# Memory attention, a mixing MLP and a gated MLP on one core: the first MLP's float64-formatted weights unpacked with one mask, the source order of the head rewritten, and the second batch's attention given later slots

## The chip, the cores and the metric

The kernel runs on one core of a Trainium2 chip. The metric is the device time of one execution in microseconds. Every time below is from the profile of one execution or from the runs of the kernel before.

## The reference, cut to what matters

Three stages follow each other, in float32, for 8 batches of 576 positions. The weights reach the chip as the 64-bit words of float64 arrays.

```python
# attention, 8 heads of 64, 32 memory slots
a = softmax(phi, axis=memory)
k_m, v_m = a.T @ k, a.T @ v                  # per head: 32 x 64
x = softmax(q @ k_m.T / 8) @ v_m             # back to 576 x 512
# first MLP
xk = mu_k * x + (1 - mu_k) * x_prev          # x_prev: the position before
xr = mu_r * x + (1 - mu_r) * x_prev
x2 = sigmoid(xr @ w_r) * (relu(xk @ w_k) ** 2 @ w_v)
# second MLP, gated over positions
h = relu(x2 @ w_in); u, v = halves(h)
out = (u * (w_spatial @ layer_norm(v) + b)) @ w_out
```

## The kernel before

**Units of work.** A batch is two attention steps (four heads each; `att_step(i)`, batch `i // 2`) and two blocks of the first MLP (288 positions each; the loop over `i` in `range(2 * B)`). A block has a K phase (8 output chunks `m`, with `w_k`), an R phase (4 chunks, with `w_r`) and a V phase (4 chunks, with `w_v`). Every product of the MLPs is made as three products of float32r halves (`three`, `gemm`, line 96), so each operand is split in a high and a low part: `split` (lines 103 and 104), a copy on ScalarE and a subtraction on VectorE. `prep_x` mixes a position with the one before it and splits the result (lines 374, 378, 103, 104).

**Weights.** `load_f64` loads 128 x 512 of the 64-bit words into a stage buffer and makes float32 of them; one such load is called a unit here. `w_k` is 8 units, `w_r` 4, `w_v` 8. There are four stage buffers in turn (`st0`, `st1`, and two halves of the tile `xT1`), and a load waits until the unit that used its buffer is done. A unit is: ScalarE scales the upper word in place (line 123); the last bits of the lower word go into place, on ScalarE in units 1 to 6 (line 127), by a shift on VectorE from unit 7 on (line 129); VectorE writes the sign into a byte (line 131) and joins both words (line 135); then a copy on ScalarE (line 141) and a subtraction on VectorE (line 142) make the two halves.

**Order.** The string `ORDER` writes the head of the kernel: `A I C K M B D L Q R q r` are loads of the first two attention steps, `w` is one unit of `w_k` (its load and its unpacking), and `a` and `b` are one stage each of attention steps 0 and 1. Behind it the four `prep_x` of block 0's K phase are made. `FIRST_BLOCK` does the same behind each chunk of block 0: `r` and `v` are units of `w_r` and `w_v`, `x` one `prep_x` of block 0's R phase. The source order is no fixed order of the engines: a planner of the framework lays out each engine's queue before the run, and takes the earliest in the source among the instructions that are ready by its own estimate. So the source order acts as a priority. Within an engine, and in SP's queue of DMA issues, the order laid out is then kept.

**Later attention.** Steps 2 to 15 are one generator, `att`; `pump`, called 20 times a block (a slot), takes pieces of it: none in slots 0 to 6, two a slot up to slot 31, then one. A step has 20 pieces. Steps 2 to 15 share one set of buffers (`space`), and step `i` issues the loads of step `i + 1` in its 12th piece. `prep_x` of a batch's first block runs in the R and V phases of the block before it.

Of the kernel before, what the change touches and what calls it, by code (L numbers as in the profile page):

```python
# [8 lines left out]
F32 = mybir.dt.float32  # L9
F32R = mybir.dt.float32r  # L10
U32 = mybir.dt.uint32
U8 = mybir.dt.uint8
ACTF = mybir.ActivationFunctionType
ALU = mybir.AluOpType
# [5 lines left out]
DM, DFF = 512, 1024  # L20
# [8 lines left out]
KC = DM // 128  # L29
# [1 line left out]

ORDER = "AICKMBDwLQRwwqwraaawaaabbbabaabbwbbwbw"


FIRST_BLOCK = ["arxxab", "b", "rxabr", "xab", "", "", "", "rv", "vvvv", "v", "", "vv"]
# [3 lines left out]
def kernel(  # L41
# [18 lines left out]
    nc = tc.nc  # L60
    scale = 1.0 / float(D) ** 0.5
# [5 lines left out]
    def tile_of(tag, shape, dtype=F32):  # L67
        return sb.tile(shape, dtype, tag=tag, name=tag)
# [16 lines left out]
    def pair(tag, shape):  # L85
        return tile_of(tag + "h", shape, F32R), tile_of(tag + "l", shape, F32R)

    def operand(n):

        return tile_of(f"xs{n}", [128, 2 * HB if n == 7 else 4 * HALF], F32R)  # L90
# [11 lines left out]
    def split(x, h, lo):  # L102
        nc.scalar.activation(out=h, in_=x, func=ACTF.Copy)  # L103
        nc.vector.tensor_tensor(out=lo, in0=x, in1=h.bitcast(F32), op=ALU.subtract)  # L104

    stages = []
    units = [0]

    def load_f64(src, wh=None, wl=None, raw=None):


        c, f = src.shape[1], src.shape[2] // 2
        buf = stages.pop(0)
        stages.append(buf)
        if isinstance(buf, str):
            buf = tile_of(buf, [128, 1024], U32)
        st = buf[:, 0:2 * c * f].rearrange("p (c f b) -> p c f b", c=c, b=2)
        nc.sync.dma_start(out=st.rearrange("p c f b -> p c (f b)"), in_=src)
        low, top = st[:, :, :, 0], st[:, :, :, 1]
        by = buf.bitcast(U8)[:, 0:8 * c * f].rearrange("p (c f b) -> p c f b", c=c, b=8)  # L120


        nc.scalar.activation(out=top.bitcast(F32), in_=top.bitcast(F32), func=ACTF.Copy, scale=2.0**-112)
        units[0] += 1
        if units[0] <= 6:

            nc.scalar.activation(out=low, in_=by[:, :, :, 3], func=ACTF.Copy, scale=2.0**-5, bias=-0.4999)
        else:
            nc.vector.tensor_scalar(out=low, in0=low, scalar1=29, scalar2=None, op0=ALU.logical_shift_right)

        nc.vector.tensor_scalar(  # L131
            out=by[:, :, :, 3], in0=by[:, :, :, 7], scalar1=128.0, scalar2=128.0, op0=ALU.is_ge, op1=ALU.mult
        )
        out = top if raw is None else raw.bitcast(U32)
        nc.vector.scalar_tensor_tensor(  # L135
            out=out, in0=top, scalar=3, in1=low, op0=ALU.logical_shift_left, op1=ALU.bitwise_or
        )
        v = out.bitcast(F32)
        if wh is None:
            return v  # L140
        nc.scalar.activation(out=wh, in_=v, func=ACTF.Copy)  # L141
        nc.vector.tensor_tensor(out=wl, in0=v, in1=wh.bitcast(F32), op=ALU.subtract)

    def weight(src, dst, n_c, width):

        chunks = src.bitcast(U32).rearrange("(c p) f -> p c f", p=128)
        for f0 in range(0, width, 128):
            for c in range(0, n_c, 4):
                load_f64(
                    chunks[:, c:c + 4, 2 * f0:2 * f0 + 256],  # L150
                    dst[0][:, c:c + 4, f0:f0 + 128], dst[1][:, c:c + 4, f0:f0 + 128],
                )
                yield
# [16 lines left out]
    def att_space(f, q, o, n, w, r):  # L170

        ns = SimpleNamespace(q=q)
        at = [0]

        def cut(t, n):
            at[0] += n
            return t[:, at[0] - n:at[0]]

        ns.kv = cut(f, NT * HG * KV).rearrange("p (t j c) -> p t j c", t=NT, j=HG)
        ns.ph = cut(f, NT * 128).rearrange("p (t m) -> p t m", t=NT)  # L180
        ns.pT = cut(f, S)
        ns.kmT = cut(f, 128)
        at[0] = 0
        ns.st = cut(o, S).rearrange("p (a m) -> p a m", m=32)
        ns.at = cut(o, S)
        at[0] = 0
        ns.vb = cut(w, 256).rearrange("p (j d) -> p j d", j=HG)
        at[0] = 0
        ns.km = cut(n, 128)
        ns.mx, ns.rs = cut(n, 1), cut(n, 1)  # L190
        ns.mx2, ns.sm = (cut(n, NBLK).rearrange("p (a m) -> p a m", m=1) for _ in range(2))
        at[0] = 0
        ns.vbh, ns.vbl = (cut(r, 256).rearrange("p (j d) -> p j d", j=2) for _ in range(2))
        ns.ats = cut(r, 2 * S).rearrange("p (j s) -> p j s", j=2)
        return ns
# [161 lines left out]
    def pump():  # L357
        n = slot[0]
        slot[0] += 1
        for _ in range(0 if n < 7 else 2 if n < 32 else 1):  # L360
            next(att, None)
        next(more[0], None)

# [5 lines left out]
    def prep_x(i, which, c):  # L369
        b, hf = divmod(i, 2)  # L370
        x32 = tile_of(next(x32_tags), [128, HB])
        n = which * KC + c

        nc.scalar.activation(
            out=x32, in_=xT[b][:, c, hf * HB:(hf + 1) * HB], func=ACTF.Copy,
            scale=mu_sb[:, 2 * KC + n:2 * KC + n + 1],
        )
        nc.vector.scalar_tensor_tensor(  # L378
            out=x32, in0=xT[b][:, c, 1 + hf * HB:1 + (hf + 1) * HB], scalar=mu_sb[:, n:n + 1], in1=x32,
            op0=ALU.mult, op1=ALU.add,  # L380
        )
        both = operand(n)[:, 0:2 * HB]
        h, lo = both[:, 0:HB], both[:, HB:]
        split(x32, h, lo)
        xs[i, which, c] = (h, lo)

    q_and_more = tile_of("ATl", [128, 4096])
    q0 = q_and_more[:, 0:HG * HB].rearrange("p (j s) -> p j s", j=HG)
    q1 = tile_of("kh", [128, HG, HB])
    n_r = 2 * HG * 64 + 2 * S  # L390
    rest = q_and_more[:, HG * HB:]
    spaces = [
        att_space(
            tile_of("ATh", [128, 4096]), q0, rest[:, 0:2 * S], rest[:, 2 * S:2 * S + 256],
# [8 lines left out]
    stages += ["st0", "st1"] + [spare[:, n, :] for n in range(2)]  # L403
    wk = pair("W1", [128, KC, DFF])
    wr = pair("W2", [128, KC, DM])
    w_k_steps = weight(w_k, wk, KC, DFF)
    w_r_steps = weight(w_r, wr, KC, DM)

    def load(n, i, late):
        dst, src = operands(i)[n + late]  # L410
        nc.sync.dma_start(out=dst, in_=src)
# [4 lines left out]
    def stage(steps):  # L416
        while not next(steps, True):
            pass

    for c in ORDER:  # L420
        if c == "w":
            next(w_k_steps)
        elif c in "ab":
            stage(first[c == "b"])
        elif c == "I":
            nc.sync.dma_start(out=ident_sb, in_=ident)
        elif c == "M":
            nc.sync.dma_start(out=mask_sb, in_=blockmask)
            nc.sync.dma_start(out=mu_sb[:, 0:2 * KC], in_=mu)
            nc.vector.tensor_scalar(  # L430
                out=mu_sb[:, 2 * KC:], in0=mu_sb[:, 0:2 * KC], scalar1=-1.0, scalar2=1.0,
                op0=ALU.mult, op1=ALU.add,
            )
        else:
            n, late = "ACKQBDLR".index(c.upper()), c.islower()
            load(n % 4, n // 4, late)
    for c in range(KC):
        prep_x(0, 0, c)

    wv = []  # L440

# [22 lines left out]
    def w_in_steps():  # L464
# [17 lines left out]
        for half in range(2):  # L482
            for j in range(2):
                load_f64(part(0, half, j), raw=quads[:, half, :, 128 * j:128 * j + 128])
                yield
                yield
# [4 lines left out]
        for j in range(2):  # L491
            at = []
            for half in range(2):
                at.append(load_f64(part(1, half, j)))
                yield
            (a11, a12), (a21, a22) = ((v[:, 0:2], v[:, 2:4]) for v in at)
            h, lo = (p[:, :, :, 128 * j:128 * j + 128] for p in wi_v)
            raw = room[:, 0:768].rearrange("p (q c f) -> p q c f", q=3, c=2)
            add(raw[:, 0], a21, a22, ALU.add)
            add(raw[:, 1], raw[:, 0], a11)  # L500
            add(raw[:, 2], a11, a21)
            for q, a in ((0, a11), (1, a12), (2, a22), (3, raw[:, 0]), (4, raw[:, 1]), (5, raw[:, 2])):
                split(a, h[:, q], lo[:, q])
                if q % 2:
                    yield
            add(raw[:, 0], a12, raw[:, 1])
            split(raw[:, 0], h[:, 6], lo[:, 6])
            yield
# [107 lines left out]
    for i in range(2 * B):  # L616
# [47 lines left out]
        for m in range(KC):  # L664
# [13 lines left out]
            n = HB if hf == 0 else 2 * HALF - HB  # L678
# [317 lines left out]
```

## Time and profile before

| | us |
|---|---|
| median of 3 runs (lowest, highest) | 1038.59 (1038.25, 1040.73) |
| profiled execution | 1039.12 |
| its span | 1037.3 |
| TensorE (PE) busy, share of the span | 989.4, 95% |
| VectorE (DVE) busy | 693.3, 67% |
| ScalarE (ACT) busy | 605.5, 58% |

The span runs from the first to the last instruction of the profile; the execution's own time is 1.82 us longer. PE's granted clock was at full speed in nearly the whole span. An engine's busy time counts overlapping instructions once.

### The profile page before, as it was taken

Reading aid. Unit: us, or ns where it says so; the run is one execution under the profiler, and the core shown is the slowest. Engines: PE = TensorE matmul, PEld = TensorE weight load, DVE = VectorE, ACT = ScalarE, POOL = GpSimd, SP = SyncE. Lnnn points to the kernel's source line nnn. Section 1 sums busy time; section 2 is a strip of 40 time slices with the busy share of each in tenths; the row PEclk is TensorE's granted clock in tenths of the full one; section 3 lists DMA queues with packets and bytes.
Section 4 is the critical chain, followed back from the end, with each engine's and each line's share of the span. In section 5 each row is a group of like instructions: output and inputs, shape, how many; then the busy total and the mean of one; then the engine's idle time right before and its main releaser. Section 6 shows DMA issues by size and latency. Waiting matters only on the chain.

```text
span 1037.3 us, 20311 instructions
## 1 busy us (share of the span) xinstructions
PE 989.4 (95%) x8080; PEld 957.8 (92%) x8080; DVE 693.3 (67%) x1558; ACT 605.5 (58%) x1287; POOL 117.3 (11%) x128
## 2 busy tenths in 40 slices
PE   3698999999999999999999999899999999999998
PEld 1387899999999999999999999899999999999998
DVE  3999956755674566567588557885665757575653
ACT  2797875675676568566766574655353534445342
POOL 0000000000000000000013022232232313132220
PEclk9999999999999999999999999899999999999999
DMA  9856622321332233223042212112110111111101
GB/s 258 260 155 205 203 80 64 113 88 55 108 111 88 58 110 105 75 66 105 7 145 64 74 44 84 39 55 65 36 61 30 59 35 53 40 59 46 54 24 46
DMA packets 67454, 88.94 MB, mean 86 GB/s; under 512 B 9504, under 2 KB 61088, under 8 KB 65312
## 3 DMA queue, kind: packets, MB, share of 16 engines
q1 hardware_dynamic: 67360, 87.65, 27.2%
q8 instruction: 63, 1.03, 0.4%
q14 instruction: 31, 0.25, 0.1%
HBM read 68.75 MB, written 18.87 MB: 84 GB/s over the span
## 4 chain that ended last, share of the span: by engine, by line
PE 81%; DVE 9%; DMA 4%; ACT 4%; issue 1%; SPq 1%; POOL 0%; ACTq 0%; POOLq 0%; DVEq 0%
PE bank L96 78%; PE bank L235 2%; DMA ATl<-in_qT 1%; DMA st<-in_w_in 1%; PE bank L285 1%; DVE xs L104 1%; DVE kl L104 1%; DMA ATh<-in_kv 1%; DVE st L131 1%; DVE xT L135 1%; DMA st<-in_w_v 0%; DVE xT L131 0%; ACT st L750 0%; ACT xs L103 0%; POOL st L558 0%
## 5 line engine op out<-in xcount | busy, mean ns | idle before, releaser
L96 PE MATMUL bank<-xs,W1h 128*128 128x288 f32 (+1 forms) x1496 | 251.9, 295 | 9.8 <-ACT xs L103 8.6
L96 PEld LDWEIGHTS bank<-xs,W1h 128*128 128x128 f32 x1496 | 214.4, 190 | 15.1 <-ACT xs L103 10.4
L96 PE MATMUL bank<-xs,W1l 128*128 128x288 f32 (+1 forms) x748 | 136.9, 292 | 0.0
L104 DVE TENSOR_TENSOR kl<-t,kh 128x576 fp32r<-128x576 f32 x64 | 49.1, 767 | 110.4 <-ACT kh L103 109.7
L96 PEld LDWEIGHTS bank<-xs,W1l 128*128 128x128 f32 x748 | 112.3, 190 | 0.0
L630 ACT ACTIVATE t<-bank 128x288 f32<-128x288 f32 x128 | 51.6, 403 | 78.3 <-PE bank L96 77.4
L767 DVE TENSOR_TENSOR st<-bank,st 128x256 f32<-128x256 f32 x90 | 37.5, 424 | 73.5 <-PE bank L96 64.9
L96 PE MATMUL bank<-kh,W3h 128*128 128x288 f32 x512 | 78.9, 295 | 6.2 <-ACT W3h L141 5.0
L96 PE MATMUL bank<-xs,W2h 128*128 128x288 f32 x512 | 84.2, 300 | 0.0
L96 PE MATMUL bank<-kh,W3l 128*128 128x288 f32 x512 | 81.3, 297 | 0.0
L96 PE MATMUL bank<-ATh,xs 128*128 128x256 f32 x472 | 75.1, 281 | 3.2 <-ACT st L770 3.1
L96 PEld LDWEIGHTS bank<-kh,W3h 128*128 128x128 f32 x512 | 71.1, 188 | 7.4 <-ACT W3h L141 5.9
L96 PE MATMUL bank<-kl,W3h 128*128 128x288 f32 x512 | 77.7, 294 | 0.0
L96 PEld LDWEIGHTS bank<-kh,W3l 128*128 128x128 f32 x512 | 71.3, 188 | 6.2 <-issue 6.0
L96 PEld LDWEIGHTS bank<-xs,W2h 128*128 128x128 f32 x512 | 72.6, 188 | 2.4 <-ACT t L630 2.2
L96 PEld LDWEIGHTS bank<-kl,W3h 128*128 128x128 f32 x512 | 71.0, 188 | 0.0
L96 PEld LDWEIGHTS bank<-ATh,xs 128*128 128x128 f32 x472 | 64.6, 191 | 3.7 <-ACT st L770 3.3
L104 DVE TENSOR_TENSOR xs<-st,xs 128x512 fp32r<-128x512 f32 x56 | 52.3, 935 | 16.1 <-ACT xs L103 16.1
L103 ACT ACTIVATE xs<-st 128x512 fp32r<-128x512 f32 x56 | 34.2, 630 | 46.0 <-POOL st L558 35.5
L103 ACT ACTIVATE kh<-bank 128x288 fp32r<-128x288 f32 x64 | 25.9, 406 | 50.9 <-DVE bank L887 50.9
L908 ACT ACTIVATE o<-bank 128x288 f32<-128x288 f32 x64 | 25.8, 404 | 45.2 <-PE bank L96 38.2
L331 POOL MEMSET xT<- 128x4 f32 x8 | 0.8, 105 | 445.0 <-DVE x32b L378 353.8
(242 smaller groups left out, 2217.4 us busy)
## 6 DMA issues: line engine op xcount, KB each, us to landing
ATh<-in_kv SPq DMA_DIRECT2D x15, 1300.0 KB, 6.1
out_T<-o SPq DMA_DIRECT2D x64, 144.0 KB, 1.7
ATl<-in_qT SPq DMA_DIRECT2D x30, 288.0 KB, 4.3
st<-x2d SPq DMA_DIRECT2D x32, 256.0 KB, 3.4
ATh<-in_phin SPq DMA_DIRECT2D x15, 320.0 KB, 3.0
x2d<-o SPq DMA_DIRECT2D x32, 144.0 KB, 2.0
ATh<-in_phiT SPq DMA_DIRECT2D x15, 288.0 KB, 2.8
st<-in_w_in SPq DMA_DIRECT2D x8, 512.0 KB, 4.0
```

Of the source, the lines that this page charges most:

```text
L96: nc.tensor.matmul(out=out, lhsT=pairs[i][0], rhs=pairs[i][1], start=i == 0, stop=i == n - 1)
L103: nc.scalar.activation(out=h, in_=x, func=ACTF.Copy)
L104: nc.vector.tensor_tensor(out=lo, in0=x, in1=h.bitcast(F32), op=ALU.subtract)
L131: nc.vector.tensor_scalar(out=by[:, :, :, 3], in0=by[:, :, :, 7], scalar1=128.0, scalar2=128.0, op0=ALU.is_ge, op1=ALU.mult)
L135: nc.vector.scalar_tensor_tensor(out=out, in0=top, scalar=3, in1=low, op0=ALU.logical_shift_left, op1=ALU.bitwise_or)
L235: nc.tensor.matmul(out=kvp[32 * j:32 * j + 32, :], lhsT=ph[:, t, 32 * j:32 * j + 32], rhs=kv[:, t, j, :], start=(t == 0), stop=(t == NT - 1),)
L285: nc.tensor.matmul(out=scs[hf][32 * j:32 * j + 32, :], lhsT=kmT[64 * hf:64 * hf + 64, 32 * j:32 * j + 32], rhs=q[64 * hf:64 * hf + 64, j, ...
L331: nc.gpsimd.memset(xT[b][:, :, 0:1], 0.0)
L630: nc.scalar.activation(out=ks[:, m % 2 * HB:(m % 2 + 1) * HB], in_=acc, func=ACTF.Relu)
L767: engine.tensor_tensor(out=dst, in0=x, in1=y, op=ALU.add)
L908: nc.scalar.activation(out=o, in_=acc, func=ACTF.Copy)
```

## The change

Three edits, with block 0's tables (`FIRST_BLOCK`) left as they are.

1. `load_f64` is cut in two: `fetch` issues the load, the rest unpacks. In units 1 to 20 (all of `w_k`, `w_r`, `w_v`) the scaled upper word now goes into one of two separate tiles (`moved`, in free room of `ATl`); ScalarE writes the last bits, as a byte, into the lowest byte of the upper word; and one VectorE mask keeps sign and last bits of that word at once. The join takes the scaled copy and the masked word. Later units (`w_in`, `w_out`) are made as before.
2. `ORDER` now issues four loads of `w_k` with the attention loads (`W`), then holds the stages of attention steps 0 and 1, then the four `prep_x` (`x`) between their last stages, and behind all of that the eight unpackings (`w`), each of which issues one more load.
3. `pump` takes no attention pieces in slots 0 to 16, and then three a slot up to slot 31.

```diff
-ORDER = "AICKMBDwLQRwwqwraaawaaabbbabaabbwbbwbw"
+ORDER = "AICKMBDWLQRWWWqraaabbbaabababaaxxbbbxxwwwwwwww"
...
+    def fetch(src):
...
+        return buf, st, c, f
+
+    def load_f64(src, wh=None, wl=None, raw=None):
+        buf, st, c, f = src if isinstance(src, tuple) else fetch(src)
         low, top = st[:, :, :, 0], st[:, :, :, 1]
...
-        nc.scalar.activation(out=top.bitcast(F32), in_=top.bitcast(F32), func=ACTF.Copy, scale=2.0**-112)
         units[0] += 1
-        if units[0] <= 6:
-            nc.scalar.activation(out=low, in_=by[:, :, :, 3], func=ACTF.Copy, scale=2.0**-5, bias=-0.4999)
+        if units[0] <= 20:
+            t = moved[units[0] % 2].rearrange("p (c f) -> p c f", c=c)
+            nc.scalar.activation(out=t, in_=top.bitcast(F32), func=ACTF.Copy, scale=2.0**-112)
+            nc.scalar.activation(out=by[:, :, :, 4], in_=by[:, :, :, 3], func=ACTF.Copy, scale=2.0**-5, bias=-0.4999)
+            nc.vector.tensor_scalar(
+                out=top, in0=top, scalar1=0x80000007 - 2**32, scalar2=None, op0=ALU.bitwise_and
+            )
+            t, low = t.bitcast(U32), top
         else:
+            t = top
+            nc.scalar.activation(out=top.bitcast(F32), in_=top.bitcast(F32), func=ACTF.Copy, scale=2.0**-112)
             nc.vector.tensor_scalar(out=low, in0=low, scalar1=29, scalar2=None, op0=ALU.logical_shift_right)
-        nc.vector.tensor_scalar(
-            out=by[:, :, :, 3], in0=by[:, :, :, 7], scalar1=128.0, scalar2=128.0, op0=ALU.is_ge, op1=ALU.mult
-        )
+            nc.vector.tensor_scalar(
+                out=by[:, :, :, 3], in0=by[:, :, :, 7], scalar1=128.0, scalar2=128.0, op0=ALU.is_ge, op1=ALU.mult
+            )
         out = top if raw is None else raw.bitcast(U32)
         nc.vector.scalar_tensor_tensor(
-            out=out, in0=top, scalar=3, in1=low, op0=ALU.logical_shift_left, op1=ALU.bitwise_or
+            out=out, in0=t, scalar=3, in1=low, op0=ALU.logical_shift_left, op1=ALU.bitwise_or
         )
...
-        for _ in range(0 if n < 7 else 2 if n < 32 else 1):
+        for _ in range(0 if n < 17 else 3 if n < 32 else 1):
             next(att, None)
...
+    moved = [q_and_more[:, 3072 + 512 * n:3584 + 512 * n] for n in range(2)]
...
+    def fetch_w_k():
+        f0 = 256 * len(fetched)
+        if f0 < 2 * DFF:
+            fetched.append(fetch(w_k_src[:, :, f0:f0 + 256]))
+
+    w_k_parts = iter(range(0, DFF, 128))
+    xk_chunks = iter(range(KC))
...
-        if c == "w":
-            next(w_k_steps)
+        if c == "W":
+            fetch_w_k()
+        elif c == "w":
+            f0 = next(w_k_parts)
+            load_f64(fetched[f0 // 128], *(t[:, :, f0:f0 + 128] for t in wk))
+            fetch_w_k()
+        elif c == "x":
+            prep_x(0, 0, next(xk_chunks))
...
-    for c in range(KC):
-        prep_x(0, 0, c)
```

## Rows read from the trace of the kernel before

**Rows 1.** The page, busy time of TensorE: us, share of the span, instructions.
```profile
PE 989.4 (95%) x8080; PEld 957.8 (92%) x8080; DVE 693.3 (67%) x1558; ACT 605.5 (58%) x1287; POOL 117.3 (11%) x128
```
**Rows 2.** Busy time by stretch: start and end, length, then us by engine.
```profile
0.00:25.00 25.00, 7.77 (x91) 4.73 (x91) 8.62 (x21) 5.44 (x10) 0.31 (x5) 1.00 0.95 257
25.00:47.40 22.40, 11.62 (x45) 5.87 (x45) 21.61 (x49) 17.78 (x37) 0.00 (x0) 1.00 0.87 256
47.40:69.00 21.60, 21.35 (x141) 20.60 (x142) 21.56 (x50) 20.84 (x46) 0.00 (x0) 1.00 0.55 160
69.00:93.65 24.65, 17.55 (x163) 15.46 (x163) 24.11 (x55) 18.38 (x35) 0.10 (x1) 1.00 0.83 257
25.00:93.65 68.65, 50.52 (x347) 41.94 (x348) 67.28 (x152) 57.01 (x115) 0.10 (x1) 1.00 0.75 226
93.65:160.00 66.35, 65.38 (x598) 60.70 (x597) 53.62 (x123) 53.27 (x115) 0.10 (x1) 1.00 0.40 128
160.00:520.00 360.00, 360.00 (x3083) 346.39 (x3082) 220.14 (x477) 233.41 (x494) 0.52 (x5) 1.00 0.26 82
```
**Rows 3.** TensorE's waits from 25 to 94 us: total, times, longest.
```profile
PE bank L96 <- ACT xs L103: 8.6, 2, 5.6
PE bank L96 <- ACT W3h L141: 5.0, 3, 2.6
```
**Rows 4.** The chain of waits, 0 to 110 us: start, us, what.
```profile
49.19 0.66 DVE st L131
...
50.90 0.58 ACT W2h L141
...
54.92 0.34 DVE st L129
...
75.37 5.07 DMA st<-in_w_v
```
**Rows 5.** VectorE's groups by shape, 0 to 94 us: busy us, mean ns.
```profile
L131 DVE TENSOR_SCALAR st<-st 128x512 uint8<-128x512 uint8 x10 | 7.6, 759 | 1.2 <-ACT st L127 1.2
...
L135 DVE SCALAR_TENSOR_TENSOR st<-st 128x512 uint32<-128x512 uint32 x10 | 6.9, 691 | 0.0
...
L129 DVE TENSOR_SCALAR xT<-xT 128x512 uint32<-128x512 uint32 x8 | 3.3, 434 | 0.0
```
**Rows 6.** ScalarE's groups by shape, 0 to 94 us.
```profile
L127 ACT ACTIVATE st<-st 128x512 uint32<-128x512 uint8 x4 | 2.7, 663 | 0.0
```
**Rows 7.** ScalarE in order of time, 70 to 84 us.
```profile
70.38 0.52 ACT L374 ACTIVATE x32b<-xT,mu 128x288 f32<-128x288 f32 x1
70.92 1.28 ACT L228 ACT_TABLE_LOAD   x1
72.21 0.74 ACT L228 ACTIVATE ATh<-ATh 128x640 f32<-128x640 f32 x1
...
76.10 1.28 ACT L651 ACT_TABLE_LOAD   x1
...
83.69 0.63 ACT L265 ACTIVATE asp<-ATl 64x128 fp32r<-64x128 f32 x2
```
**Rows 8.** TensorE in order of time, 54 to 86 us.
```profile
54.22 1.23 PE L96 MATMUL bank<-xs,W1h 128*128 128x288 f32 x8
...
55.82 1.23 PE L96 MATMUL bank<-xs,W1h 128*128 128x288 f32 x8
...
73.00 1.32 PE L235 MATMUL bank<-ATh 128*32 128x130 f32 x40 [2.08 <-ACT ATh L228]
...
85.38 0.72 PE L285 MATMUL bank<-ATl,ATh 64*32 64x288 f32 x16
```
**Rows 9.** SP's queue of DMA issues in order of time.
```profile
20.90 9.32 SPq L118 DMA_DIRECT2D st<-in_w_k  x2
...
81.52 0.37 SPq L118 DMA_DIRECT2D st<-in_w_in  x1
```
**Rows 10.** VectorE in order of time: attention step 2 begins, step 3 ends.
```profile
67.23 0.77 DVE L221 TENSOR_REDUCE ATl<-ATh 128x1 f32<-128x576 f32 x1
...
118.01 1.54 DVE L325 TENSOR_TENSOR asp<-ATl,asp 64x576 fp32r<-64x576 f32 x2
```

More of the change, by code (lines that the diff above doesn't have):

```diff
@@ L107 @@
     units = [0]
-    def load_f64(src, wh=None, wl=None, raw=None):
+    def fetch(src):
         c, f = src.shape[1], src.shape[2] // 2
@@ L405 @@
     wr = pair("W2", [128, KC, DM])
-    w_k_steps = weight(w_k, wk, KC, DFF)
+    w_k_src = w_k.bitcast(U32).rearrange("(c p) f -> p c f", p=128)
+    fetched = []
+    def fetch_w_k():
[4 more added lines that the diff above has]
+    xk_chunks = iter(range(KC))
     w_r_steps = weight(w_r, wr, KC, DM)
```

## The prediction

> **What bounds the kernel now.** Read the busy times of the page first: TensorE is busy 989.4 of 1037.3 us [rows 1], so 47.9 us of the span are all that any reordering can win. The table by stretch then shows where they lie. From 160 to 520 us TensorE has no gap at all; up to 93.65 us, the end of block 0's V phase, it stands idle 17.2 + 10.8 + 0.25 + 7.1 = 35.4 us, from there to 160 us 1.0, and behind 520 us some 11.6 [rows 1, 2]. The head alone is at stake, and in it the question is which engine sets the pace. Up to 25 us the DMA engines are nearly full (share 0.95), and what has not arrived cannot be unpacked. From 25 to 93.65 us VectorE is busy 67.3 of 68.65 us, ScalarE 57.0, TensorE 50.5 [rows 2]. So VectorE is the bound of this stretch. The waits agree: TensorE stands longest for the last operand of block 0's K phase (8.6 us in two waits) and then for the halves of `w_v` (5.0 in three) [rows 3]; both end with ScalarE, but the chain of waits runs through VectorE's unpacking, with one DMA piece of 5.07 us at 75.37 [rows 4].
>
> **The change, part by part.** Instructions in a full queue overlap a little, so I price them by their share in the chain: sign byte 0.66 us, shift 0.34, ScalarE's copy of the same size 0.58 [rows 4]; alone they last 0.76, 0.43 and 0.66 [rows 5, 6].
>
> *The mask, VectorE's side.* All 20 units lose the sign byte; 14 lose the shift; all gain one mask. No mask is in the trace. It has the form of the shift (one 32-bit source, 128x512, in place), so I take 0.34; the bounds are that and the sign byte's 0.66. Units 7 to 20 save 0.66 + 0.34 - 0.34 = 0.66 each, units 1 to 6 save 0.32: 9.2 + 1.9 = 11.2 us. At the upper bound 6.4 of these are lost. The join keeps its form and its 0.69 us [rows 5]; one of its sources is now contiguous, which no row prices apart, and which I count as nothing. VectorE then has 67.3 - 11.2 = 56.1 us of work where it had 67.3, or 62.5 at the bound.
>
> *The mask, ScalarE's side.* Fourteen units that had no byte copy now have one. The trace has it with a 32-bit output, 0.66 us alone [rows 6]; with a byte output it is not shown. I take the same 0.58 in a full queue: 14 x 0.58 = 8.1 us more. The lower bound is the same number (nothing in the trace is cheaper at this size); for the upper bound I let a byte output cost ScalarE what bytes cost VectorE against words, 0.76 to 0.43 [rows 5], which makes 1.1 us of it, 20 x 0.47 = 9.4 us more. The scaling keeps its source and size, and I count the new place of its output as nothing. The two `moved` tiles let ScalarE run two units ahead, enough to hide their reuse while VectorE is no longer full; with VectorE full, each join would hold the next scaling but one.
>
> *Attention pushed back.* In block 0 TensorE now does none of attention step 2, which before had its 40 matmuls at 73.00 and its 16 at 85.38 there, 1.32 + 0.72 = 2.0 us [rows 8]. That work is not gone: it comes back behind block 0. ScalarE loses the step's exponential and two copies, 0.74 + 0.63 = 1.4 us, and with them two table loads: one at 70.92 ahead of that exponential and one at 76.10 back to the sigmoid, 2 x 1.28 = 2.6 us [rows 7]. The next exponential starts at 72.21, at the load's end, and the one at 70.92 begins where the instruction of 70.38 ends, so a switch costs 1.28 here and no more. The Trainium skill ("ScalarE: Activation LUTs", What ACT_TABLE_LOAD costs) states a drain of about 1.38 us with each load, 2.66 for a switch; by that the two switches would give back 5.3 us and the time would be 2.7 us lower, but this trace disagrees. Step 3's loads, which are issued inside step 2, move behind `w_v`'s units as well; I count that into ScalarE's smaller idle time below.
>
> *The order of the head.* The loads `W` go to SP one place earlier than the last two attention loads, so the first of those (step 0's second half of `q`) lands behind one more unit; only second-half scores need it, and block 0's K phase needs first halves alone: nothing. Units 5 to 8 are issued behind unpackings 1 to 4 as the four buffers allow, which is where SP stood 9.3 us before, too [rows 9]. The stages of steps 0 and 1 and their `prep_x` now go ahead of the unpacking on both engines, so the 8.6 us for K's operands should shrink to a few. I add no term for it: K's chunks then come at the pace of the unpacking, and the end of block 0 is set by the sum of the work on the fullest engine.
>
> *The sum.* ScalarE now has 57.0 + 8.1 - 2.6 - 1.4 = 61.1 us from 25 us to the end of V, VectorE 56.1 or less: ScalarE becomes the bound. Its own idle time in that stretch was 11.6 us, mostly waits for a full VectorE; from 47.4 to 69 us, where it was best fed, 0.76 of 21.6, or 3.5% [rows 2]. I take 3.5% of 61.1, 2.1 us, and 2.3 us at the end, in which TensorE still works on the last unit (one subtraction, 0.7 us as the join [rows 5], and half a V chunk: a K chunk of 12 matmuls takes 55.82 - 54.22 = 1.6 us [rows 8], a V chunk has 24). V then ends at 25 + 61.1 + 4.4 = 90.5, which is 3.15 us earlier. From this go 2.0 us of attention that are still to do. Against it, TensorE can fill waits in V with K chunks of block 1, whose operands are no longer last on a full VectorE: none to three chunks of 1.6 us, as banks come free; I take half, 2.4 us. The net is 3.15 - 2.0 + 2.4 = 3.55 us. The span would be 1033.75 us and the profiled execution 1035.6; the median of the runs shown lies 0.5 us under the profiled execution, so 1035.0.
>
> **The rivals.** A measurement of this kernel can tell about 0.3%, 3.1 us, from no change: under 1035.5 is faster, over 1041.7 slower.
>
> *Both engines well fed.* With attention out of the way ScalarE's waits nearly vanish (1 us in place of 2.1), K's operands come some 8 us earlier and three K chunks fit in V's gaps. For it: the DMA piece of 5.07 us [rows 4] goes when step 3's loads don't stand between `w_v`'s. That gives 4.25 - 2.0 + 4.8 = 7 us, 1031.5; with byte copies that start before 25 us, 1028.
>
> *ScalarE takes it all back.* Byte copies cost more than 0.58, or exponentials still land between the sigmoids (plus 2.6), and V's gaps cannot be filled (plus 2.4): 1040.0; at the byte copy's upper bound 1044.4. For it: ScalarE was already busy 20.8 of 21.6 us from 47.4 to 69 [rows 2]. The Trainium skill (the same page, Rules for kernel authors) would keep plain arithmetic off ScalarE. By that rule the byte copies are on the wrong engine; the rows say 0.66 against 0.43 us for one, so it agrees on the price, and only which engine is full decides.
>
> *Attention is late (the other side).* Steps 2 and 3 must be done before block 2's K phase. They start at slot 17, in V's third chunk, about 86 us, and block 1 takes 20 x 1.6 = 32 us and some 4 for an attention step, to about 126; less 3 for `prep_x`, that leaves 37 us. Before, they ran from 67.23 to 119.6, 52 us [rows 10]. If they keep more than 37 us, TensorE waits for the rest at block 2: at the old pace 15 us, at three quarters of it 11 - 3.55 above today, 1046. For it: with three pieces a slot, 39 are issued by slot 30, just what the third `prep_x` there needs; before it was 46. Against it: the 52 us had a full VectorE, TensorE waited only 1.0 us behind 93.65 [rows 2], and the engines' order follows readiness, not slots: SP issued a load of `w_in` at 81.52, in block 0 [rows 9], though its source stands behind block 12. In later blocks the shift of five slots puts an exponential next to the sigmoids, two more table loads a block at most; ScalarE is busy 233 of 360 us there [rows 2], so they are hidden.
>
> **Chances.** Forecast 0.45 (1032 to 1038, a little over half of it faster), both well fed 0.20, ScalarE takes it back 0.20 (three quarters the same), attention late 0.15 (nearly all slower). Faster 0.24 + 0.20 = 0.44, the same 0.21 + 0.15 + 0.02 = 0.38, slower 0.05 + 0.13 = 0.18. The range 1028 to 1043 takes in the first three but for the byte copy's upper bound, and leaves out most of the last.
>
> **What would show it.** Right: masks of 0.34 to 0.45 us, byte copies near 0.66, VectorE clearly under ScalarE from 25 us to V's end, that end near 90, one sigmoid table load in block 0, full K matmuls from about 39 us. Wrong: byte copies near 1 us; V's end behind 93; TensorE waiting for `prep_x` or an attention copy at 115 to 130 us; new waits between 160 and 520 us.

## The result, and the profile after

The changed kernel takes 1045.87 us (median of 6 runs, 1044.31 to 1047.76); the kernel before 1040.43 (6 runs, 1038.25 to 1042.43). The ratio is 1.0056 [1.0039, 1.0073]: slower by some 5.8 us, where 1035.0 was forecast, in 1028 to 1043. In what follows a ratio is always to the kernel before, measured beside the run, with a 95% interval in brackets; 0.001 is 1.04 us.

The page after: span and busy times, to be read against [rows 1].

```profile
span 1042.5 us, 20345 instructions
...
PE 997.6 (96%) x8080; PEld 964.5 (93%) x8080; DVE 687.8 (66%) x1544; ACT 653.6 (63%) x1323; POOL 117.8 (11%) x128
```

TensorE has the same 8080 instructions and is busy 8.2 us longer: some of them ran more slowly. The stretches show where; columns as in [rows 2].

```profile
40.00:45.00 5.00, 5.00 (x23) 4.23 (x18) 3.94 (x9) 5.00 (x10) 0.00 (x0) 0.50 0.92 351
...
55.00:60.00 5.00, 2.57 (x12) 1.93 (x12) 4.50 (x11) 5.00 (x10) 0.00 (x0) 0.89 0.32 105
60.00:65.00 5.00, 4.39 (x19) 4.04 (x18) 4.03 (x8) 4.61 (x12) 0.00 (x0) 0.50 0.33 105
...
25.00:93.65 68.65, 50.96 (x278) 44.24 (x279) 56.50 (x121) 67.52 (x120) 0.00 (x0) 0.88 0.64 193
...
25.00:99.12 74.12, 56.43 (x345) 48.98 (x346) 61.83 (x136) 71.92 (x129) 0.22 (x2) 0.88 0.61 182
```

Two things have changed places. From 25 to 93.65 us VectorE is busy 56.50 us, where it had 67.28, and ScalarE, with 67.52 of 68.65, is the full engine. And TensorE's granted clock, 1.00 throughout this stretch before [rows 2], is 0.88 here; 0.50, that is 1.2 in place of 2.4 GHz, from 40 to 45 and from 60 to 65 us. V's last product ends at 99.12 us; before, the next one started at 93.65.

The groups by shape, 0 to 100 us (line, engine, operation, tiles, shapes, count, busy us, mean ns; then the idle time ahead), beside [rows 5] and [rows 6]:

```profile
L135 ACT ACTIVATE xT<-xT 128x512 uint8<-128x512 uint8 x10 | 13.8, 1381 | 0.0
...
L149 DVE SCALAR_TENSOR_TENSOR xT<-ATl,xT 128x512 uint32<-128x512 uint32 x10 | 6.9, 688 | 0.1
...
L136 DVE TENSOR_SCALAR xT<-xT 128x512 uint32<-128x512 uint32 x10 | 4.3, 430 | 5.3 <-ACT xT L135 5.3
```

The mask (L136) lasts 0.43 us and the join (L149) 0.69, both as forecast. The byte copy (L135) lasts 1.38 us, where the copy with a 32-bit output lasted 0.66 [rows 6]. The idle time ahead of the masks ends with that copy, 5.3 us for these ten. In the chain of waits from 40 to 100 us each one has 1.22 to 1.27 us, against the 0.58 of [rows 4]:

```profile
44.91 1.27 ACT xT L135
...
49.62 0.55 ACT ATl L134
50.59 1.25 ACT st L135
...
59.25 1.24 ACT xT L135
```

TensorE's waits from 25 to 100 us, to be read against [rows 3], end with ScalarE but for 0.4 us; those for `w_v` (W3h) have grown from 5.0 in three to 6.2 in six, and `w_r` (W2h) has joined them.

```profile
PE bank L97 <- ACT W3h L155: 6.2, 6, 2.3
PE bank L97 <- ACT asp L104: 4.5, 1, 4.5
PE bank L97 <- ACT W2h L155: 3.4, 3, 1.9
```

### The profile page after: what moved, and what is told of

Read it like the earlier page. It is cut to its first block, busy times and chain, and to the rows that moved or that the text cites. A ratio compares the mean times of both kernels' runs of the same rounds, so it can differ in the third digit from the quotient of the medians.

```text
span 1042.5 us, 20345 instructions
## 1 busy us (share of the span) xinstructions
PE 997.6 (96%) x8080; PEld 964.5 (93%) x8080; DVE 687.8 (66%) x1544; ACT 653.6 (63%) x1323; POOL 117.8 (11%) x128
## 4 chain that ended last, share of the span: by engine, by line
PE 78%; ACT 10%; DVE 6%; DMA 3%; issue 1%; POOL 1%; SPq 1%; DVEq 0%; ACTq 0%; POOLq 0%
PE bank L97 75%; PE bank L249 2%; ACT xT L135 1%; ACT st L135 1%; DMA W3h<-in_kv 1%; DMA st<-in_w_in 1%; ACT ATl L134 1%; ACT xs L104 1%; DVE xs L105 1%; PE bank L299 1%; ACT kh L104 1%; DVE kl L105 0%; ACT t L660 0%; ACT x32a L388 0%; ACT x32b L388 0%
## 5 line engine op out<-in xcount | busy, mean ns | idle before, releaser
L97 PE MATMUL bank<-xs,W1h 128*128 128x288 f32 (+1 forms) x1496 | 248.1, 294 | 3.4 <-ACT W1h L155 1.3
L97 PE MATMUL bank<-kh,W3h 128*128 128x288 f32 x512 | 83.6, 303 | 6.2 <-ACT W3h L155 6.2
L105 DVE TENSOR_TENSOR xs<-x32a,xs 128x288 fp32r<-128x288 f32 x64 | 29.1, 454 | 67.8 <-ACT xs L104 67.6
```

The lines of the kernel that those rows point to most:

```text
L97: nc.tensor.matmul(out=out, lhsT=pairs[i][0], rhs=pairs[i][1], start=i == 0, stop=i == n - 1)
```

## The experiments

### One part alone

The unpacking, the order and the slots were taken out or put in one at a time.

Old unpacking in the changed kernel (new order and later attention stay):

```diff
-        if units[0] <= 20:   # scaled copy aside, byte copy, mask
+        if units[0] <= 6:    # top scaled in place; these copy the last bits, later ones shift; sign byte by VectorE
...
```

> The changed kernel's source order and its later attention, with the unpacking of the kernel before. Theory 1 (the loss of block 0 is ScalarE's byte copy, which lasts 1.38 us with a byte output where 0.66 was priced): ScalarE has some 18 us less before the end of V, VectorE bounds again but without attention step 2's work, V ends near 90 us where the change had 99, and the time is 1037 to 1041 us. Rival (the new order and the later attention cost the time themselves): within 2 us of the changed kernel, 1044 or more.

Measured 1045.53 us, 1.0037 [1.0018, 1.0056], the rival's time. So order and slots alone lose 3.8 us. The new unpacking on top of them adds 0.0019, and the intervals of the two overlap.

The unpacking alone, in the kernel before:

```diff
-        nc.scalar.activation(out=top.bitcast(F32), in_=top.bitcast(F32), ...)   # and shift, sign byte
+        if units[0] <= 20: t = moved[units[0] % 2] ...   # scaled copy aside, byte copy, mask
...
```

> The kernel before with the mask alone: old order, old attention slots. Theory 1: ScalarE gets 14 byte copies of about 1.1 us more and 6 that are 0.5 longer, 18 us on top of 57 from 25 us on, which is more than that stretch holds; V ends 8 to 11 us later than before, and the time is 1047 to 1052 us. Rival (order and attention cost it): VectorE's relief shows, 1040 or less.

1048.48 us, 1.0070 [1.0045, 1.0094]; V ends at 105.9.

The changed kernel with the old slots:

```diff
-        for _ in range(0 if n < 17 else 3 if n < 32 else 1):
+        for _ in range(0 if n < 7 else 2 if n < 32 else 1):
```

> The changed kernel with the attention slots of the kernel before (mask and new source order stay). Theory 1: ScalarE stays the bound; attention step 2 returns into block 0 with 1.4 us and up to two table loads on a full ScalarE, while its 2 us on TensorE are done in waits, and the later blocks lose their 0.16 us each: 1043 to 1047. Rival (the later attention is the cost): back to 1040 or less.

1048.07 us, 1.0071 [1.0047, 1.0095]. With the old slots the kernel with the new unpacking stands 7 us behind in either order. With the later attention it is 5.8; the intervals overlap.

The order alone (old unpacking, old slots), and the later attention alone:

```diff
-ORDER = "AICKMBDwLQRwwqwraaawaaabbbabaabbwbbwbw"          # order alone
+ORDER = "AICKMBDWLQRWWWqraaabbbaabababaaxxbbbxxwwwwwwww"
...
-        for _ in range(0 if n < 7 else 2 if n < 32 else 1):   # later attention alone
+        for _ in range(0 if n < 17 else 3 if n < 32 else 1):
```

> The kernel before with the new source order of the head alone (old unpacking, old attention slots). Theory 2 (the order starts block 0's K phase early, VectorE still needs the same work before the end of V, and TensorE, which now runs out of units after a part of K, falls to half its clock and does the next matmuls at 0.24 to 0.27 us): V ends no earlier than before, 1040 to 1045 us. Rival (order is harmless, the later attention made the run with old unpacking slow): 1036 to 1040 us, V ending before 91 us.

> The kernel before with the later attention slots alone. Theory 2: VectorE loses attention step 2's 6.7 us before the end of V, so V ends 3 to 6 us earlier; 2 us of matmuls come later, and the later blocks pay their 0.16 us each and the place where attention meets the units of the second MLP's weights: 1038 to 1042 us. Rival (attention comes late in block 1 and TensorE waits for it): 1043 or more, with waits for an attention load or copy at 100 to 130 us.

Order 1044.32, 1.0041 [1.0027, 1.0054]; later attention 1041.79, 1.0012 [0.9997, 1.0026]. Their sum, 0.0053, agrees with the 1.0037 of the first run within the intervals. The forecast had priced the order at nothing, and had counted on a gain from the later attention in block 0, with 2.0 us of products moved behind it and no cost in the later blocks.

### The width of ScalarE's output

The last bits written as a 32-bit word in place of `low`; VectorE then needs a sign mask with a second source in place of the plain mask:

```diff
-            nc.scalar.activation(out=by[:, :, :, 4], in_=by[:, :, :, 3], ...)
-            nc.vector.tensor_scalar(out=top, in0=top, scalar1=0x80000007 - 2**32, ..., op0=ALU.bitwise_and)
+            nc.scalar.activation(out=low, in_=by[:, :, :, 3], ...)
+            nc.vector.scalar_tensor_tensor(out=top, in0=top, scalar=2**31, in1=low,
+                                           op0=ALU.bitwise_and, op1=ALU.bitwise_or)
```

> The changed kernel, but ScalarE writes the last bits as 32-bit words, as the first units of the kernel before did, and VectorE joins the sign bit to them with one and-or of three operands in place of the mask. Theory 1: the copies last 0.66 us again, ScalarE has 20 x 0.5 = 10 us less and VectorE 20 x 0.26 = 5 us more, V ends 6 to 9 us earlier than in the changed kernel, and the time is 1036 to 1040 us. Rival: no more than 2 us below the changed kernel.

1041.31 us, 1.0001 [0.9984, 1.0018], a little over the 1036 to 1040 expected. The groups by shape of that run:

```profile
L135 ACT ACTIVATE xT<-xT 128x512 uint32<-128x512 uint8 x10 | 6.9, 687 | 0.4 <-DMA xT<-in_w_k 0.4
L136 DVE SCALAR_TENSOR_TENSOR st<-st 128x512 uint32<-128x512 uint32 x10 | 6.8, 684 | 0.5 <-ACT st L135 0.4
```

The copy is back at 0.69 us although VectorE's part costs 0.68 in place of 0.43, and 5.7 us of the loss are gone. The source is the same byte, and the output has the same stride of 8 bytes; only its width differs. A 16-bit output (into the lower half of the upper word, mask as changed):

```diff
-            nc.scalar.activation(out=by[:, :, :, 4], in_=by[:, :, :, 3], ...)
+            nc.scalar.activation(out=by2[:, :, :, 2], in_=by[:, :, :, 3], ...)   # by2: the buffer as 16-bit words
```

> The changed kernel, but ScalarE writes the last bits as a 16-bit word into the lower half of the upper word (the mask then clears bits 8 to 15 of it, which are zero); everything else as changed. Theory 1 (the slow copy is a matter of the byte as output type): the copy lasts 0.66 us as with 32 bits, VectorE keeps its 0.43 us mask, V ends at 91 to 94 and the time is 1037 to 1041. Theory 2 (any output narrower than 32 bits at a stride of 8 bytes is slow): the copy stays at 1.1 to 1.4 us and the time at 1044 to 1047.

1048.40 us, 1.0070 [1.0057, 1.0083], with copies as slow as the byte's:

```profile
L136 ACT ACTIVATE xT<-xT 128x512 uint16<-128x512 uint8 x10 | 13.6, 1364 | 0.0
```

So it is not the byte as a type: both outputs narrower than 32 bits cost twice as much here. Whether a narrow output without gaps would cost as much was not tried.

The 32-bit copy was also tried with the old slots (`0 if n < 7 else 2 if n < 32 else 1`), in the new order and, put into the kernel before, in the old one:

> The changed kernel with the 32-bit copy, and the attention slots of before: new order and unpacking alone. If the effects of the three parts add up (word unpacking against old unpacking in the new order -4, later attention +1): 1040. If later attention is what lets the unpacking gain (as ScalarE has no exponentials in block 0 then): 1043 to 1046.

> The kernel before with the word-output unpacking alone in units 1 to 20 (old order, old slots). ScalarE 14 x 0.58 = 8.1 us more than before and VectorE 14 x 0.40 = 5.6 us less: theory 1 with both engines near full: 1037 to 1042 us. Rival (the separate scaled tiles or the third operand cost more than the copies): 1043 or more.

New order 1040.78, 1.0002 [0.9985, 1.0018]; old order 1045.77, 1.0044 [1.0027, 1.0062]. With the old unpacking the new order loses 4 us, with this one it gains 4. The parts don't add up, and the reason of this sign was not settled: in the old order the time is that of the rival, but whether the separate scaled tiles or the third operand cost it was not tried.

### What the order costs: the clock, or late units

In the order-only kernel K's operands are ready early, so its chunks follow the unpacking unit by unit. Its windows from 45 us:

```profile
45.00:50.00 5.00, 4.25 (x32) 4.02 (x31) 4.97 (x13) 4.25 (x9) 0.00 (x0) 1.00 0.99 229
50.00:55.00 5.00, 3.06 (x13) 3.06 (x14) 4.46 (x10) 3.00 (x6) 0.00 (x0) 0.62 1.02 256
55.00:60.00 5.00, 2.33 (x8) 1.58 (x7) 5.00 (x14) 4.94 (x12) 0.00 (x0) 0.50 0.49 161
60.00:65.00 5.00, 4.02 (x14) 3.47 (x15) 4.78 (x11) 4.38 (x11) 0.00 (x0) 0.50 0.33 105
65.00:70.00 5.00, 5.00 (x29) 5.00 (x27) 4.70 (x9) 4.30 (x9) 0.00 (x0) 0.68 0.32 105
```

TensorE is busy 3.06, then 2.33 of 5 us, the granted clock goes to 0.50, and it is still 0.68 while TensorE is full again from 65 to 70 us. Seven of K's eight chunks are done by then, at a clock of 1.00. What falls into these windows is the last chunk, which waits for the last unit of `w_k` (W1), and behind it the R phase (W2); TensorE in order of time:

```profile
51.94 1.33 PE L97 MATMUL bank<-xs,W1h 128*128 128x288 f32 x4 [2.69 <-ACT W1h L147]
...
54.98 0.68 PE L97 MATMUL bank<-xs,W2h 128*128 128x288 f32 x2
```

Before, TensorE was full from 47.4 to 69 us, in K and the start of R, at 1.00 [rows 2]. Two orders were made to tell the clock from the lateness of the units: all four `prep_x` behind the unpackings, and the unpackings back between the attention stages.

```diff
-ORDER = "AICKMBDWLQRWWWqraaabbbaabababaaxxbbbxxwwwwwwww"
+ORDER = "AICKMBDWLQRWWWqraaabbbaabababaabbbwwwwwwwwxxxx"   # prep_x last
+ORDER = "AICKMBDWLQRWWWqrwwwwaaawaaabbbabaabbwbbwbwxxxx"   # units early, prep_x last
```

> The order-only kernel (old unpacking, old attention slots, new order: 1044.3), but with the four prep_x of block 0's K phase behind the eight unpackings of w_k. Theory 1 (the new order loses because the K phase starts early, is fed unit by unit and runs at the lower granted clock): K starts near 47 and runs at a clock of 1.00, the 4 us come back, 1040 to 1042. Theory 2 (it loses because the attention stages go ahead of the unpackings and every unit is later): units are as late as in the order-only kernel, 1043 to 1046.

> The order-only kernel with the unpackings of w_k back at their old places between the attention stages, and the prep_x last; only the early issue of four loads of w_k is left of the new order. Theory 1 and theory 2 both expect about the time before, 1039 to 1042; a time at 1044 would put the loss on the early loads.

`prep_x` last: 1042.42, 1.0011 [0.9998, 1.0024]; units early too: 1041.74, 1.0010 [1.0000, 1.0019]. Moving `prep_x` alone takes back 3 us of the order's 4, with the same stages ahead of the same unpackings. The profile of the first of these runs does not show how: in it TensorE is full from 50 to 65 us at a clock of 1.00, but that execution, 1045.04 us, is the slowest of its twelve and no better than the profiled one of the order-only kernel (1045.21), and V ends at 101.2 us, where it ended at 100.3. And the same move with the 32-bit copy went the other way:

> The changed kernel with the 32-bit copy (1041.3), with the four prep_x of block 0's K phase behind the eight unpackings of w_k. Theory 1 (early K phase at a low clock costs): 1037 to 1039, faster than before. Theory 2 (the units' lateness costs, and prep_x later only starts K later): 1041 to 1044.

1044.43, 1.0025 [1.0011, 1.0038], against 1.0001 with `prep_x` early. In that profile the clock is 1.00 from 50 to 70 us, and 0.83 from 70 to 80; but the profiled execution took 1041.57, 2.9 us less than the median, so it does not tell what the others lost. Starting K late is no remedy by itself. The next experiment leaves the order alone and gives TensorE something to do: products that the chunk's own first product overwrites.

```diff
             ms = slice(m * 128, (m + 1) * 128)
+            for _ in range(10 if i == 0 and m > 0 else 0):
+                nc.tensor.matmul(out=acc, lhsT=wk[0][:, 0, 0:128], rhs=xk[0][0], start=True, stop=True)
             gemm(acc, three(
```

> The order-only kernel (1044.3) with ten extra matmuls ahead of each K chunk 1 to 7 of block 0, on chunk 0's operands, into the bank that the real products then overwrite: 70 x 0.134 = 9.4 us of TensorE work at full clock, ready long before the real operands. Theory 1 (the fed-by-the-unit K phase runs at the lower granted clock, and that costs the 4 us): the clock stays at 1.00 from 45 to 75 us, the extra work fits into the idle time, 1040 to 1044. Theory 2 (units and queue places are late, the clock only fills idle time): the extra work costs as much as in the kernel before or more, 1045 to 1051.

> The kernel before with the same extra matmuls, the control: its clock is 1.00 already and its K phase is full from 47 to 69 us, so the extra work can only be hidden behind the waits for w_r and w_v (some 5 to 8 us). Both theories: 1041 to 1049, and no gain.

> The changed kernel with the 32-bit copy (1041.3), with the same extra matmuls. Its clock was 0.66 from 55 to 75 us. Theory 1: 1037 to 1041. Theory 2: 1042 to 1048.

> The changed kernel itself (byte output) with the same extra matmuls. If the low clock accounts for about as much here as with the 32-bit copy or in the order-only kernel (2 to 3.6 us): 1042 to 1044, and what is left against the filled kernel with the 32-bit copy, 4 to 6 us, is the byte output alone. If ScalarE, full from 35 to 95 us, sets V's end whatever the clock: 1045 to 1047.

The order-only kernel went from 1.0041 [1.0027, 1.0054] to 1.0006 [0.9990, 1.0022] (1040.99 us), with an estimated 9.4 us more work on TensorE. The control, the kernel before, stayed: 1039.47 us, 0.9992 [0.9978, 1.0007], less than either theory allowed; all of the extra work was hidden there. The windows of the filled order-only kernel:

```profile
50.00:55.00 5.00, 5.00 (x40) 5.00 (x39) 5.00 (x15) 3.34 (x8) 0.00 (x0) 1.00 0.64 196
55.00:60.00 5.00, 4.41 (x31) 3.95 (x30) 5.00 (x12) 5.00 (x13) 0.00 (x0) 1.00 0.39 130
60.00:65.00 5.00, 4.36 (x31) 4.07 (x30) 5.00 (x10) 4.83 (x10) 0.00 (x0) 1.00 0.33 104
```

The clock stays at 1.00 in these windows. In the groups from 50 to 65 us one matmul of the same shape lasts 489 ns on average unfilled (first row) and 304 filled; matmuls overlap, so these are lengths and not costs.

```profile
L97 PE MATMUL bank<-xs,W2h 128*128 128x288 f32 x7 | 2.8, 489 | 2.9 <-ACT xs L104 2.9
```

```profile
L97 PE MATMUL bank<-xs,W2h 128*128 128x288 f32 x24 | 4.2, 304 | 0.5 <-ACT xs L104 0.5
```

The Trainium skill ("TensorE: Matmul & The Clock Gate", HAM oscillation — how this bites in real kernels) tells of a kernel whose short bursts between waits each ran at the lower clock; the order-only kernel agrees, at 0.50 from 55 to 65 us, behind waits of 2.69 and 2.10 us.

How much of the 3.6 us between these two kernels is the clock's stays open. The extra products also change what the planner lays out behind them, and the two profiles differ before the first extra product runs, at 32.20 us. VectorE's last instruction on the second unit of `w_k`, then on the last unit of `w_v`; unfilled, then filled:

```profile
31.30 0.69 DVE L148 TENSOR_TENSOR W1l<-st,W1h 128x512 fp32r<-128x512 f32 x1 [0.52 <-ACT W1h L147]
...
95.99 0.69 DVE L148 TENSOR_TENSOR W3l<-xT,W3h 128x512 fp32r<-128x512 f32 x1
```

```profile
28.06 0.69 DVE L148 TENSOR_TENSOR W1l<-st,W1h 128x512 fp32r<-128x512 f32 x1
...
90.51 0.70 DVE L148 TENSOR_TENSOR W3l<-xT,W3h 128x512 fp32r<-128x512 f32 x1
```

V ends some 3.6 us behind the last unit in both (100.3 and 94.9), and of the 5.5 us between their last units 3.2 were there at the second. Nor was a lower mean clock a longer time among the nine executions of the order-only kernel: the shortest, 1043.02 us, had 0.976, the longest, 1046.21, 0.992.

With the 32-bit copy the filled kernel takes 1037.85, 0.9990 [0.9972, 1.0008], against 1.0001 unfilled; a gain of 1.1 us, within the intervals. The changed kernel filled: 1046.25, 1.0060 [1.0036, 1.0084], no gain at all. Its windows from 50 us:

```profile
50.00:60.00 10.00, 8.86 (x67) 8.63 (x66) 9.27 (x24) 10.00 (x23) 0.00 (x0) 1.00 0.74 198
60.00:70.00 10.00, 9.16 (x67) 8.68 (x66) 7.66 (x15) 10.00 (x20) 0.00 (x0) 1.00 0.39 129
```

The clock is 1.00 and ScalarE is busy 10.00 of 10.00: here the byte copies set the pace whatever the clock is. Between the two filled kernels, 0.9990 and 1.0060, only the width of the output and VectorE's mask differ: 7 us.

### The slots behind block 0

The ends of the V phases tell what a later attention costs in the steady blocks. TensorE in order of time, the last V products of block 1 and of block 11; the kernel before, then later attention alone:

```profile
133.89 1.21 PE L96 MATMUL bank<-kl,W3h 128*128 128x288 f32 x8
...
491.25 1.21 PE L96 MATMUL bank<-kl,W3h 128*128 128x288 f32 x8
```

```profile
135.76 1.21 PE L96 MATMUL bank<-kl,W3h 128*128 128x288 f32 x8
...
494.56 1.21 PE L96 MATMUL bank<-kl,W3h 128*128 128x288 f32 x8
```

The lag grows from 1.87 to 3.31 us over ten blocks. The changed kernel's grows from 3.37 to 4.77 us in the same blocks; that of the order-only kernel, which has the old slots, stays at 6.07 from block 2 to block 11. In these nine blocks a block takes 35.72 us before and 35.88 with the later attention. All twenty profiles divide so: 35.87 to 35.88 in the eight with the later slots, 35.71 to 35.72 in the twelve with the old ones or with the catching up below, whatever the unpacking and the order. The 0.16 us a block are the slots' own. The sigmoid's table loads in the whole kernel are 15 before and, with later attention alone,

```profile
L651 ACT ACT_TABLE_LOAD x26 | 33.4, 1283 | 0.5
```

To undo the shift and keep block 0 free of attention, the pieces were made to catch up by slot 22:

```diff
-        for _ in range(0 if n < 17 else 3 if n < 32 else 1):
+        for _ in range(0 if n < 17 else 4 if n < 22 else 3 if n < 32 else 1):
```

> The run with word outputs, with slots 17 to 21 taking four attention pieces, so that 50 pieces are done by slot 32 as in the kernel before and the later blocks meet attention in the old phase. Theory 3 (the five slots' shift costs 0.16 us in each later block and some 1 us where the second MLP's weights begin): 1.5 to 3 us below the run with word outputs, and 15 sigmoid table loads in place of 26. Rival (the shift is hidden, as predicted): within 1 us of it.

> The kernel with 32-bit copy and extra matmuls (1037.9), with later attention that comes back to the slots of before by slot 22 (four pieces a slot in slots 17 to 21). Theory: the 0.16 us per block of the five-slot shift go, 1.7 to 2.7 us, and the lead of 2.9 us that the filled kernel's profile has at the end of block 1 lasts to the end: 1035 to 1037, faster than before by 0.3%. Against it: the earlier catching up delays block 1, 1038 to 1040, as in the same trial without the extra matmuls (1041.3 and 1041.4).

With the 32-bit copy: 1041.36, 1.0006 [0.9994, 1.0019], no better than 1.0001. The drift is gone in its trace (35.72 us a block, 16 sigmoid loads), but block 2 ends 4.1 us later than without the catching up. With the extra matmuls as well: 1037.08 us, 0.9974 [0.9956, 0.9993], 2.7 us under the kernel before and the one of nineteen versions whose interval lies below 1. The same without the catching up has 0.9990, and the intervals overlap. Its profile, TensorE's last V products of blocks 1 and 11, then a window from 45 to 70 us:

```profile
133.49 1.21 PE L97 MATMUL bank<-kl,W3h 128*128 128x288 f32 x8
...
491.44 1.21 PE L97 MATMUL bank<-kl,W3h 128*128 128x288 f32 x8
```

```profile
45.00:70.00 25.00, 22.73 (x164) 21.57 (x163) 24.54 (x51) 24.38 (x52) 0.00 (x0) 1.00 0.62 184
```

Both unpacking engines are 97% full or more there, and TensorE's clock holds. But that one execution, 1038.49 us, is slower than the run's median, and its block 11 ends 0.19 us behind the kernel before: where the 2.7 us come from is not shown, and one run this near to the edge of its interval would have to be repeated.

## Why the prediction was wrong

*The mask on VectorE: right.* 0.43 us alone, the join unchanged. The work of 56.1 us was forecast up to V's end. Up to 93.65 us it is 56.50; up to V's late end, at 99.12, it is 61.83, with 2.3 us of `w_in` units and some of attention step 2, which were not counted there.

*The byte copy on ScalarE: the term that failed.* It was priced at 0.58 us in a full queue (0.66 alone) with an upper bound of 1.1. Measured: 1.25 in the chain and 1.38 alone, beyond the bound. The bound was made from VectorE's ratio of bytes to words, 0.76 to 0.43; ScalarE's is 1.38 to 0.69. Eighteen of the twenty copies start after 25 us, and 18 x (1.25 - 0.58) = 12.1 us; ScalarE's work up to the end of V is 71.9 us where 61.1 was forecast, 10.8 more (it also holds 1.4 us of `w_in` units and 2.0 of attention step 2, so the two sums agree only roughly). V then ends at 99.1, not at 90.5. That ScalarE becomes the bound was right; how far it passes VectorE was not. In time this is 5.7 us unfilled (1.0056 against 1.0001) and 7 filled.

*With the copy at about the price forecast* (0.69 us) the change still gains nothing: 1.0001 [0.9984, 1.0018], where 1035.0 of 1038.59, or 0.9966, was forecast. So the byte copy accounts for the loss against the kernel before, and not for the gain that is missing. The 3.7 us between the old unpacking (1.0037) and the 32-bit copy (1.0001) resemble the forecast net of 3.55 by chance: that net was for all three parts, and in the old order the same unpacking loses (1.0044). Nearest to the forecast comes the 32-bit copy with the extra products: in its profile V ends at 90.9 us, where 90.5 was forecast, and block 1 ends 2.5 us ahead of the kernel before; at block 11 1.0 of these is left, and the time is 0.9990.

*Attention pushed back, in block 0: right in the main.* One sigmoid load there, and 24 K products of block 1 before V's end (120 with W1 against 96 of block 0), two chunks where one and a half were counted. Step 2 did not stay out, though: its exponential (at 93.46 us) and its 40 matmuls (94.43 to 97.34) come before V's late end.

*The order of the head, "I add no term for it": the second step that failed.* It costs 4 us with the old unpacking (1.0041). The step saw that "K's chunks then come at the pace of the unpacking", and took that as harmless because the sum of work on the fullest engine sets the end. In the order-only profile it doesn't: VectorE, the fullest, is busy 64.69 us from 25 to 93.65, less than the 67.28 of before, and yet the last unit is done 5 us later, at 96.7, and V ends at 100.3. What holds the units up was not settled. TensorE's half clock in K's last chunk and in R is one candidate, and the extra products, which keep the clock up, take 3.6 us back; other queues and a later start are the others (its second unit is done at 32.0 us, in the kernel before at 29.8). In the changed kernel itself the order costs nothing in addition: with the byte copies and the old slots the old order has 1.0070 and the new one 1.0071, and filling gains nothing.

*The shift of five slots, "hidden": the third.* The table loads were foreseen (ScalarE is busy 260.2 us from 160 to 520 in the changed kernel, against 233.4 [rows 2]) and ScalarE has room for them; yet every kernel with the later slots loses 0.16 us a block, the changed kernel 1.4 us from block 1 to block 11. TensorE there is no longer without a gap, 359.62 of 360 us from 160 to 520; what makes up the rest of the 1.4 us, the table loads or something else, was not isolated.

*Rivals.* "ScalarE takes it all back" was the nearest, with 1044.4 at its upper bound, and its first condition is what happened. "Attention is late" was not: the changed kernel's block 1 ends 3.4 us behind, less than V's end of block 0 does (5.3, last product to last product), and TensorE's waits from 100 to 145 us come to 0.8. With the old unpacking, in the same order and slots, it was, at least in the execution profiled (1046.58 us): V ends at 93.5 there, no later than before, and block 1 ends 5.6 us late; TensorE waits 2.79 us for an attention load in it, and its clock is 0.66 from 110 to 115 us. So the 3.8 us of order and slots do not lie in block 0 alone.

*Open.* Why the new order helps the 32-bit copy (1.0044 to 1.0002) and hurts the old unpacking; why `prep_x` last helps one and hurts the other. Each new order makes the planner lay out other queues. In the order-only kernel, TensorE's queue at the end of V shows such a place (TensorE in order of time):

```profile
92.61 0.80 PE L97 MATMUL bank<-kh,W3h 128*128 128x288 f32 x4 [2.02 <-ACT W3h L147]
95.68 0.85 PE L97 MATMUL bank<-xs,W1h 128*128 128x288 f32 x2 [2.28 <-DVE o L697]
96.33 1.16 PE L97 MATMUL bank<-kh,W3h 128*128 128x288 f32 x4
```

Two K products of block 1 stand ahead of V's next four and wait 2.28 us for a bank. The run with `prep_x` last has a wait of 2.3 us on the same release, so this place alone does not tell the two apart, and no run here isolates it.

## What to carry to other kernels

Before work is moved to another engine, its price there needs a row with the same output width, not only the same size; a ratio borrowed from a second engine is no bound. Where an earlier start lets a phase run in bits, look at the granted clock in windows of 5 us before calling the order free, and try extra products in the waits as a test: they cost nothing in the kernel before, and the order-only one was 3.6 us faster with them. Before two profiles are compared, line up their starts: here 3.2 us of a difference were there before the edit had run. A change to a periodic schedule is best read from the length of one period, which here told 0.16 us apart in single profiles.

## What the runs showed of the hardware

A ScalarE copy of 128x512 from strided bytes took 0.66 to 0.69 us with a 32-bit output, 1.36 with a 16-bit one and 1.38 with an 8-bit one, each at a stride of 8 bytes. With extra TensorE work, estimated at 9.4 us, one kernel was 3.6 us faster and another stayed as it was. In the order-only kernel the granted clock was 0.50 to 0.68 from 50 to 70 us; TensorE was busy 3.1 and 2.3 of 5 us in the first two of these four windows, and full in the last.
